# Moving the first stages of an attention and FFN kernel: products of zeros first, Q by head pairs, sums ahead of V, and loads issued later

## The chip, the cores and the metric

The kernel runs on one core of a Trainium2 chip. The metric is the device time of one execution in microseconds (us). The span of an execution (first to last instruction of the program) is 1.7 to 2.2 us shorter than its time.

## The reference, cut to what matters

```python
# q, k, v: (batch 8, heads 8, sequence 1024, head_dim 64); E, F: (64, 1024)
k_proj = np.einsum('ks,bhsd->bhkd', E, k)
v_proj = np.einsum('ks,bhsd->bhkd', F, v)
scores = scale * np.matmul(q, k_proj.transpose(0, 1, 3, 2))
attn = softmax(scores)                       # over the 64 projected positions
x = np.matmul(attn, v_proj)                  # reshaped to (8192 tokens, 512)
h = np.maximum(x @ w_in, 0.0)                # w_in: (512, 2048)
return h * h @ w_out                         # w_out: (2048, 512)
```

The attention is cheap and the FFN is large. The change touches only how batch 0 gets from the first load to the first FFN matmul.

## The kernel before: the parts that the change and the argument touch

All loads of K, Q, V, `w_in` and `w_out` are issued by GpSimd on one queue. The issue order is K, Q, V in three pieces, and then the weights. The first block of `w_in` comes in two pieces, `n = 0` and `n = 1`.

```python
for s in (slice(0, 4), slice(4, 8)):
    load_heads(K_first, k, s)
load_q_half(0, slice(0, H))
for s in (slice(0, 4), slice(4, 6), slice(6, 8)):
    load_heads(V_first, v, s)
# ... (cut)
for j in (0, 2, 1, 3):
    # ... (cut)
    for g in range(2):
        for n in range(2) if (j, g) == (0, 0) else (slice(None),):
            # ... (cut)
            nc.gpsimd.dma_start(
                w_in_sb[j][:, g, :, s], w_in_view[:, g, :, j * fw:(j + 1) * fw][:, :, s])
```

The first stages of batch 0 run in program order on each engine. The `filler` products are thrown away; they keep TensorE busy.

```python
def first_stages(self):
    def filler(n):                       # needs ET, so runs only once E is transposed
        ps = ffn_psum("ps_fill")
        for _ in range(n):
            nc.tensor.matmul(ps[:], lhsT=ET[:, 0:2, :], rhs=ET[:], start=True, stop=True)
    filler(2); self.project_k(0); filler(1); self.transpose_k(0)      # (lines joined here)
    self.project_k(1); filler(2); self.transpose_k(1); filler(1)
    for g in range(2):
        self.half_transpose_q(0, g, ffn_psum)
    for g in range(2):
        self.half_scores(0, g)
        self.half_exponentials(g)
    heads = [slice(0, 4), slice(4, 6), slice(6, 8)]
    self.project_v(heads[0]); self.copy_v(heads[0])
    self.half_sums(0, apart=True); self.half_sums(1)
    self.half_reciprocals(0); self.half_reciprocals(1)
    self.half_values(0)
    for s in heads[1:]:
        self.project_v(s); self.copy_v(s)
    self.half_values(1)
    # ... four normalizes, then the FFN
```

The FFN opens with four steps of four matmuls. Step `cb` needs the piece of x that one normalize writes. Steps 0 and 1 need the first block of `w_in`.

```python
if b == 0 and ch == 0:
    steps[0:4] = [
        lambda cb=cb: opening(range(4), (cb,), cb == NCB - 1) for cb in range(NCB)]
```

The softmax here doesn't subtract the row's maximum and nothing guards it: scores larger than these inputs give would overflow.

## Time and profile before

| before | value | read from |
|---|---|---|
| time | 483.68 us (483.64 to 484.29) | 3 runs |
| span of the profiled run | 482.4 us | the page |
| TensorE busy | 97% of the span | the page |
| first FFN matmul | 21.05 us | the timeline |
| FFN matmul 17 (the first 16 are done) | 24.70 us | the chain in order of time |
| first matmuls of batch 1's K and V | 53.03 and 53.32 us | the timeline |

Read it from the bottom. TensorE is nearly full from 21 us on. The two places where the first stages meet a deadline are the first FFN matmul and the projection of batch 1's K and V.

### The profile page before, as it was taken

To read this page: it belongs to the slowest core of one execution; us is meant where nothing else is said; L and a number is where in the kernel's file an instruction comes from. 1 tells how busy PE (TensorE), PEld (TensorE's weight loads), DVE (VectorE), ACT (ScalarE), POOL (GpSimd) and SP (SyncE) were. 2 spreads that over 40 slices of the span, in tenths; PEclk is the share of its full clock that TensorE was granted. 3 is DMA by queue.
4 is the path that set the end of the run, shared out by engine and by line. 5 is a ranking of instruction groups with operands and counts; after the bars stand their busy time and mean duration, and the time that the engine had idled before them with its cause. 6 is when DMAs were issued, how large, how long until landed. Compare 5 with 4: busy or idle time off the path is not lost.

```text
span 482.4 us, 8423 instructions
## 1 busy us (share of the span) xinstructions
PE 470.3 (97%) x3630; PEld 292.6 (61%) x3630; DVE 314.1 (65%) x382; ACT 261.5 (54%) x413; POOL 34.7 (7%) x48
## 2 busy tenths in 40 slices
PE   4899999999999999999999999999999999999997
PEld 2544676475574746657475665747557474666656
DVE  1478955554958559493776848667494855948383
ACT  2387544758427564466635667176662756545351
POOL 6540020020020001000010000100000000000000
PEclk9999999999999999999999999999999999999999
DMA  9999989579989086941859147690702102020202
GB/s 155 203 204 207 168 181 200 137 120 229 180 128 229 12 175 88 180 94 50 153 86 227 22 115 131 91 200 1 165 11 75 25 1 88 1 88 0 88 1 87
DMA packets 72789, 55.46 MB, mean 115 GB/s; under 512 B 33968, under 2 KB 64944, under 8 KB 72752
## 3 DMA queue, kind: packets, MB, share of 16 engines
q0 software_dynamic: 30624, 29.36, 39.4%
q1 hardware_dynamic: 42128, 25.56, 21.1%
q8 instruction: 28, 0.46, 0.4%
q14 instruction: 9, 0.07, 0.0%
HBM read 59.24 MB, written 16.78 MB: 158 GB/s over the span
## 4 chain that ended last, share of the span: by engine, by line
PE 92%; DVE 3%; DMA 3%; ACT 1%; POOL 1%; issue 0%; POOLq 0%
PE ps_h L459 44%; PE ps_y L479 23%; PE ps_z L479 11%; PE ps_x L479 6%; DMA V_sb<-in_v_dram 3%; PE ps_kv L180 2%; PE ps_att L221 2%; PE ps_att L206 2%; DVE hsq L521 1%; DVE s L473 1%; PE ps_v L284 0%; DVE xT L246 0%; DVE xT L351 0%; PE ps_kv L181 0%; ACT h_relu L513 0%; POOL K_sb L93 0%
## 5 line engine op out<-in xcount | busy, mean ns | idle before, releaser
L459 PE MATMUL ps_h<-xT,w_in 128*128 128x512 bf16 x1024 | 224.8, 379 | 0.2 <-DVE xT L351 0.2
L521 DVE TENSOR_TENSOR hsq<-h_relu 128x1024 bf16<-128x1024 f32 x123 | 149.9, 1222 | 75.0 <-ACT h_relu L513 74.2
L513 ACT ACTIVATE h_relu<-ps_h 128x512 f32<-128x512 f32 x255 | 149.4, 597 | 63.4 <-PE ps_h L459 63.0
L459 PEld LDWEIGHTS <-w_in 128*128 128x128 bf16 x1024 | 99.7, 98 | 117.7 <-issue 1.9
L479 PEld LDWEIGHTS <-s 128*128 128x128 bf16 x1024 | 98.5, 98 | 19.8 <-issue 8.7
L479 PEld LDWEIGHTS <-hsq 128*128 128x128 bf16 x768 | 73.8, 98 | 17.3 <-issue 3.8
L479 PE MATMUL ps_y<-T,s 128*128 128x256 bf16 x512 | 62.4, 273 | 0.0
L246 DVE TENSOR_TENSOR xT<-ps_att,rs 128x1024 bf16<-128x1024 f32 x28 | 33.4, 1215 | 17.6 <-ACT rs L236 17.0
L473 DVE TENSOR_TENSOR s<-hsq 128x1024 bf16<-128x1024 bf16 x64 | 43.5, 683 | 0.0
L591 ACT COPY o_sb<-ps_y 128x512 f32<-128x512 f32 x15 | 8.8, 586 | 53.8 <-PE ps_y L479 53.7
L213 ACT ACTIVATE expT<-ps_att 128x1024 bf16<-128x1024 f32 x28 | 27.2, 1025 | 14.0 <-PE ps_att L206 14.0
L479 PE MATMUL ps_x<-w_out,hsq 128*128 128x256 bf16 x256 | 33.2, 273 | 0.0
L479 PE MATMUL ps_y<-w_out,hsq 128*128 128x256 bf16 x256 | 33.2, 273 | 0.0
L595 DVE TENSOR_TENSOR o_sb<-ps_z,p_b 128x512 f32<-128x512 f32 x16 | 11.0, 688 | 33.8 <-issue 19.9
L479 PE MATMUL ps_y<-T,hsq 128*128 128x256 bf16 x256 | 30.9, 272 | 0.0
L479 PE MATMUL ps_z<-T,s 128*128 128x256 bf16 x256 | 30.6, 273 | 0.0
L479 PE MATMUL ps_z<-w_out,s 128*128 128x256 bf16 x256 | 30.6, 273 | 0.0
L591 ACT COPY p_b<-ps_y 128x512 f32<-128x512 f32 (+1 forms) x17 | 9.4, 556 | 25.9 <-PE ps_y L479 25.8
L81 POOL DMA_DIRECT2D Q_sb<-in_q_dram x7 | 6.1, 876 | 227.7 <-DMA qT<-Q_sb 227.2
L473 DVE TENSOR_TENSOR s<-s,hsq 128x1024 bf16<-128x1024 bf16 x32 | 21.8, 684 | 0.3
L473 DVE TENSOR_TENSOR s<-hsq,s 128x1024 bf16<-128x1024 bf16 x32 | 21.7, 682 | 0.0
L591 ACT COPY p_a<-ps_y 128x512 f32<-128x512 f32 (+1 forms) x17 | 9.4, 561 | 21.8 <-PE ps_y L479 21.6
(75 smaller groups left out, 233.0 us busy)
## 6 DMA issues: line engine op xcount, KB each, us to landing
out_dram<-o_sb SPq DMA_DIRECT2D x30, 512.0 KB, 3.8
K_sb<-in_k_dram POOLq DMA_DIRECT2D x7, 1024.0 KB, 15.3
V_sb<-in_v_dram POOLq DMA_DIRECT2D x7, 1024.0 KB, 22.4
Q_sb<-in_q_dram POOLq DMA_DIRECT2D x7, 1024.0 KB, 9.4
w_out<-in_moe_w_out_dram POOLq DMA_DIRECT2D x4, 512.0 KB, 13.2
w_in<-in_moe_w_in_dram POOLq DMA_DIRECT2D x7, 256.0 KB, 10.0
K_sb<-in_k_dram POOLq DMA_DIRECT2D x2, 512.0 KB, 8.5
out_dram<-o_sb SPq DMA_DIRECT2D x3, 256.0 KB, 2.1
```

What stands on the lines that cost most here:

```text
L180: nc.tensor.matmul(ps[0:KP, :], lhsT=ET[:, i, :], rhs=kv[:, :, i, :], start=f, stop=l)
L206: nc.tensor.matmul(ps[o, bank, :], lhsT=self.kT[r, 2 * pr + j, :], start=True, stop=True, rhs=self.qT[r, NT * (2 * pr + j):NT * (2 * pr + ...
L213: nc.scalar.activation(e[:], self.ps["s", pr][:], AF.Exp, scale=SCALE)
L221: nc.tensor.matmul(ps[32 * j:32 * j + 32, a, :], lhsT=weights(o, 4 * g + j), rhs=self.exp[2 * g + j // 2][o, bank, :], start=True, stop=Tr ...
L246: nc.vector.tensor_tensor(out=self.xT[:, 2 * g + e].rearrange("p a n t -> p a (n t)"), in0=self.ps["v", g, e][:], in1=self.rs[g][:], op=AL ...
L459: nc.tensor.matmul(ps[:], lhsT=w_in_blk(cb, fb), rhs=xT[:, cb, :, 2 * ch:2 * ch + 2], start=(cb == 0), stop=(cb == NCB - 1),)
L473: nc.vector.tensor_tensor(out=s[o][:, js], in0=x, in1=y, op=op)
L479: nc.tensor.matmul(ps[tb] if len(ps) == 2 else ps[0][:, tb], lhsT=lhs[:, j, tb * P:(tb + 1) * P], rhs=rhs[:, j], start=first and n == 0 an ...
L513: nc.scalar.activation(r[:, n], ps[:], AF.Relu)
L521: multiply = lambda: nc.vector.tensor_tensor(out=o, in0=r[:], in1=r[:], op=ALU.mult)
L591: nc.scalar.copy(to[:, t], ps)
L595: nc.vector.tensor_tensor(out=to[:, t], in0=ps, in1=more[:, t], op=ALU.add)
```

## The change

The intent is to have TensorE at full clock before K lands, to keep GpSimd's issues out of the way of VectorE, and to start the FFN before the last values are through. The diff, cut to its core:

```diff
     load_q_half(0, slice(0, H))
-    for s in (slice(0, 4), slice(4, 6), slice(6, 8)):
-        load_heads(V_first, v, s)
+    zeros = const_pool.tile([P, 512], BF16, name="zeros")
+    nc.vector.memset(zeros[:], 0.0)
@@ loads
+    def loads_of_v():
+        nc.gpsimd.tensor_copy(landed[:, 0:1], ET[:, 0, 0:1])     # waits for E's transposes
+        for s in (slice(0, 4), slice(4, 6), slice(6, 8)):
+            load_heads(V_first, v, s)
+    def loads_of_weights(kT):
+        nc.gpsimd.tensor_copy(landed[:, 1:2], kT[:, 0, 0:1])     # waits for kT's first half
+        ... (the loads of w_in and w_out, as before)
+    def filler(n):
+            nc.tensor.matmul(ps[:], lhsT=zeros[:, 0:P], rhs=zeros[:], start=True, stop=True)
@@ first_stages
-            filler(2)
+            filler(3)
             self.project_k(0)
-            filler(1)
+            filler(3)
             self.transpose_k(0)
+            loads_of_weights(self.kT)
             self.project_k(1)
-            filler(2)
+            filler(3)
             self.transpose_k(1)
-            filler(1)
-            for g in range(2):
-                self.half_transpose_q(0, g, ffn_psum)
+            for n in range(4):
+                self.half_transpose_q(
+                    0, range(2 * n, 2 * n + 2), ffn_psum, nc.scalar.copy if n == 1 else nc.vector.tensor_copy)
...
+            self.half_sums(0, apart=True)
             self.project_v(heads[0])
             self.copy_v(heads[0])
-            self.half_sums(0, apart=True)
...
             self.half_values(0)
+            self.half_normalize(0, 0, 0)
             for s in heads[1:]:
...
+        def last_of_first(self):                  # now called after the first FFN step
             self.half_values(1)
@@ main
+        filler(10)
         E_and_F()
+        loads_of_v()
```

## The prediction

> **What bounds the kernel now.** I read the page first, then the chain of waits in order of time, then the timeline of the two places where a load could hold TensorE, and the rates by stretch. Over the whole span the page's chain is TensorE with few breaks:
>
> ```profile
> PE 92%; DVE 3%; DMA 3%; ACT 1%; POOL 1%; issue 0%; POOLq 0%
> ```
>
> Columns of the next view, the chain in order of time: start, duration, work.
>
> ```profile
> 4.21 12.57 DMA V_sb<-in_v_dram
> 16.78 0.04 issue
> 16.82 1.06 PE ps_v L284 x16
> ...
> 19.43 0.66 PE ps_v L284 x16
> 20.09 0.02 issue
> 20.11 0.29 DVE vp L288
> 20.40 0.61 DVE xT L351
> 21.01 0.04 issue
> 21.05 3.61 PE ps_h L459 x16
> 24.67 0.04 issue
> ```
>
> The first 16.8 us are a load: V's first four heads, issued at 4.21, land 12.57 us later. From 19.43 to 21.05 a short serial tail follows (project the last two heads of V, copy, normalize), then the FFN starts. So the diff works on at most the first 21 us; from there TensorE is nearly full.
>
> Is the load late because it is issued late, or because it queues? The stretches (columns: window, length, busy time of PE, PEld, DVE, ACT, POOL, clock, DMA share, GB/s) say the latter:
>
> ```profile
> 4.00:9.00 5.00, 2.21 (x18) 1.29 (x18) 1.11 (x2) 1.63 (x2) 4.02 (x6) 1.00 1.10 163
> 9.00:20.00 11.00, 9.74 (x141) 6.16 (x141) 3.86 (x10) 3.72 (x7) 3.90 (x6) 1.00 1.32 202
> 20.00:50.00 30.00, 29.52 (x219) 13.33 (x216) 24.55 (x31) 21.67 (x37) 8.12 (x11) 1.00 1.26 205
> ```
>
> From 9 to 50 us the loads run at a flat 202 to 205 GB/s, whatever the engines do. By issue plus landing time the order is strictly K, Q, V, w_in: K's halves at 8.7 and 11.6, Q at 14.2, V at 16.8, 18.2, 19.4, w_in from 20.0, each 256 KB taking about 1.27 us. One queue is full all the way.
>
> The decisive lines come much later, where batch 1's K and V are first used:
>
> ```profile
> 30.31 0.88 POOL L81 DMA_DIRECT2D V_sb<-in_v_dram  x1 [0.40 <-PE ps_att L307]
> ...
> 53.03 0.40 PE L180 MATMUL ps_kv<-K_sb,ET 128*64 128x512 bf16 x1
> 53.03 0.11 PEld L181 LDWEIGHTS <-FT 128*64 128x64 bf16 x1
> ...
> 53.32 0.38 PE L181 MATMUL ps_kv<-V_sb,FT 128*64 128x512 bf16 x1
> ```
>
> The tile view gives 23.0 us from issue to landing for that V: 30.31 + 23.0 = 53.3. The weights of V's projection are in the array at 53.03, with K's first matmul, but V's first matmul starts at 53.32. One batch later, where the loads are long done, both start together:
>
> ```profile
> 92.79 0.40 PE L180 MATMUL ps_kv<-K_sb,ET 128*64 128x512 bf16 x1
> 92.79 0.11 PEld L181 LDWEIGHTS <-FT 128*64 128x64 bf16 x1
> 92.79 0.40 PE L181 MATMUL ps_kv<-V_sb,FT 128*64 128x512 bf16 x1
> ```
>
> So at 53.3 us TensorE has just caught up with the load queue and already waits about 0.29 us. Whatever it gains before is waited away here, unless the queue itself gets ahead. That is the step on which I stake the prediction.
>
> **What the Trainium skill says.** (1) "DMA: Bandwidth & Descriptors", section Queues, rings and completion order: on each DMA engine descriptors are consumed in ring order. The trace agrees: loads land in the order of issue. Holding back a later issue then does nothing for an earlier load, as long as the ring does not run dry. (2) "TensorE: Matmul & The Clock Gate", Part 1, the clock gate: TensorE runs at half clock until busy for about 3.4 us. The trace shows the effect: the eight matmuls of K's first half took 1.92 us from 9.11, those of the second half 1.06 us from 12.00. (The granted clock shows as 1.00 throughout, so the durations decide.) (3) "SBUF — State Buffer", section Who interferes with whom: VectorE's two-port copies and GpSimd's descriptor writing share a port, and the later one waits. Compatible: of V's three issues two took about 0.71 us and one 1.02, with VectorE's cast of E from 4.24 to 4.93 beside it.
>
> **The change part by part.**
>
> *Zeros and filler.* Ten 128x512 products before E: cold ones run at roughly 0.43 us (twice the warm 13.81 / 64 = 0.216), so about 4.3 us from near 1.4, after a memset that I estimate at 0.5 us (ones: 0.09 for 32 columns). They end near 5.7, so E's transposes move from 4.98 to about 5.7 and ET from 6.14 to 6.9. K lands only at 8.7: no loss. TensorE is warm for K's first half: 1.92 becomes 1.06, and kT's first half is ready near 11.3 instead of 12.4. But K's second half lands at 11.6 and Q at 14.2, so Q's transposes still start at 14.2 to 14.3. Worth 0.
>
> *V's loads after E, w_in's after kT.* V is issued at about 7 instead of 4.2. The ring holds K and Q until 14.2, so it does not run dry: V lands at 16.8 as before. Seven w_in issues of 0.70 us from about 11.5 are in the ring by about 16.5, before V's last load at 19.4: w_in lands as before. Worth 0. Two one-column GpSimd copies (an estimate, 0.2 us each) are off the path.
>
> *Q by head pairs.* Before, two copies of 128x1024 of 0.69 us, and the first scores at 15.69. After, four of 128x512: 0.42 on VectorE (as ET's copy), 0.59 on ScalarE (as FT's copy). From 14.27: pair 0 done at 15.1, pair 1 (ScalarE) 15.5, pairs 2 and 3 15.6 and 16.0. Scores start at 15.6 and 16.05 instead of 15.69 and 16.29; the exponentials end at 18.0 instead of 18.1. Worth 0.1.
>
> *Sums ahead of V.* V's projection now waits for the first exponentials (17.05) and the sums: 17.2 to 18.3, where it had 16.82 to 17.88. The values come near 18.8 instead of 18.4, still before the reciprocals (near 19.3). Not on the path.
>
> *First FFN step before the last values.* The first normalize (0.62 us) is done near 20.0, so the first four FFN matmuls (0.9 us) start when V's last projection ends, near 20.1, instead of at 21.05, and cover the copy. Then values (0.45), and the 12 other matmuls. The first 16 end at 20.1 + 3.6 + 0.45 + 0.05 = 24.2, against 24.66. The loads allow it, just: w_in's third block lands at 22.1, and its fifth at 24.6 is wanted at 24.65.
>
> Sum on TensorE before 53 us: about 0.45 us earlier. On the span: TensorE reaches batch 1's projection at about 52.6, V lands at 53.3 all the same, the wait grows from 0.29 to about 0.7, and the end moves by 0 to 0.1 us.
>
> **Rivals.** *A, the queue gets faster.* Between 4 and 9 us it moved 163 GB/s, not 203: 5 x 40 KB = 200 KB, 1.0 us. GpSimd issues without a break until 8.0 in that stretch. If that writing slows the transfers, and the later issue cures it, the landing at 53.3 comes forward by up to 1 us and the gain on TensorE counts as well: 482.7 to 483.2. Against: GpSimd is idle from 8 to 9 and the rate is still low, and from 20 to 21.8 it issues without a break at 210 GB/s. *B, TensorE bound after all,* with the reading at 53.3 wrong: 483.68 - 0.45 = 483.2. *C, a new wait.* w_in's issues, back to back, meet VectorE's two-port kp copy at 13.5 and hold it up to 0.7 us, and with it, in order, Q's transposes. Up to +0.5 on the first stages, for which the wait at 53.3 has some 0.7 of room: 483.7. *D, the ring runs dry,* if GpSimd's first copy is very slow (over 5 us before V's issue) or waits for a late ET: +1 to +3. Nothing in the profile speaks for it.
>
> **Range and chances.** Main line 483.6; A and B together have perhaps a third and pull down by 0.5, D is rare. I say 483.5, with 482.9 to 484.2 for eight times in ten; the runs before alone spread from 483.64 to 484.29. Two per cent would be 9.7 us; the touched stretch has 21 us, of which 16.8 are a full queue. Same 0.985, faster 0.008, slower 0.007.
>
> **What would show it.** Right: batch 1's V still lands at about 53.3; its first matmul starts there, with K's first well before it (0.6 us or more); first FFN matmul near 20.1, the first 16 done near 24.2; Q's transposes at 14.3; K's first projection about 1.1 us long. Wrong: V's landing earlier than 53.0 (A), no wait on it at all (B), Q's transposes later than 14.6 (C), a hole in the load rate between 12 and 20 us (D).

## More of the kernel before

All runs told of here count as fast-state runs.

The columns are packets, MB, and share of 16 engines' span.

```profile
q8 instruction: 28, 0.46, 0.4%
```

These are 28 packets of 16 KB that carry instructions. They move 0.46 MB beside 55 MB of data, so they look like nothing.

Executions of one kernel on this core scatter by about 2 us: 43 runs of the kernel before, on several chips, lie between 483.30 and 485.74.

## The result, and the profile after

The changed kernel took 484.81 us (median; 484.31 to 485.01, 6 runs), and the kernel before took 483.81 us (483.52 to 484.58, 6 runs) in the same rounds. The ratio is 1.0016, with a 95% interval of 1.0003 to 1.0029. Ratios here are the mean time of one kernel's fast runs over that of the other's of the same rounds, so not quite the ratio of the medians quoted. A later set of five runs of the unchanged diff gave 484.36 and 1.0005. Taken together, 11 runs after average 484.60 and 43 runs before average 484.10. The change therefore costs about half a microsecond, 0.1%. The time was above the predicted range, and nothing was gained.

Most of that half microsecond lies outside the span, so the profiles here do not show it. Time minus span is 1.71 to 1.81 us in all 37 runs of the kernel before for which it is listed, and 2.09 to 2.16 us in the 11 runs after: 0.36 us more on average, and the two groups do not overlap. The mean spans are 482.35 before and 482.47 after; the 0.12 between them is lost in the scatter. Where the 0.36 us come from was not tested. defer_only (1.78 on average) has none of it, fillers_only and ten_zeros (2.0) have part of it, and every kernel with the new order (2.08 to 2.22 in 50 runs, those of no_filler among them) has it all. What follows explains the two profiled executions, whose spans happen to be 0.45 us apart.

The page's chain is still TensorE, 92% of the span as before. The stretches (columns as in the prediction: window, length, busy time of PE, PEld, DVE, ACT, POOL, clock, DMA share, GB/s) show the same load rate from 9 us on (202 GB/s, and 205 from 20 to 50 us, as before). The view now shows a granted clock below 1:

```profile
4.00:9.00 5.00, 3.67 (x23) 1.66 (x21) 1.11 (x2) 1.63 (x2) 2.60 (x5) 0.86 1.10 160
9.00:20.00 11.00, 9.54 (x133) 6.02 (x134) 4.11 (x11) 4.39 (x8) 5.15 (x9) 0.91 1.31 202
```

This does not mean that the kernel before had the better clock here. The view shows 1.00 until the first change of clock that the trace holds, and in the kernel before that is the rise at 11.2 us; K's first half took 1.92 us there, as at half clock. For the same reason the mean granted clock of a run counts only what is lost after the first rise: no_filler's profiled run has 1.000, although it is at half clock to 23.26 us.

The chain in order of time (start, duration, work) no longer runs through V. It runs through K, kT, the issue of `w_in`, and a piece of `w_in`:

```profile
9.25 1.89 PE ps_k L278 x8
...
12.58 0.18 POOL landed L127
12.77 0.63 POOL w_in L134
13.39 8.20 DMA w_in<-in_moe_w_in_dram
21.59 0.05 issue
21.63 0.60 PE ps_h L476 x2
```

The timeline of TensorE shows what that piece does. The bracket gives the idle time before a line and what ended it.

```profile
20.39 0.61 PE L476 MATMUL ps_h<-xT,w_in 128*128 128x512 bf16 x2
21.63 0.60 PE L476 MATMUL ps_h<-xT,w_in 128*128 128x512 bf16 x2 [0.64 <-DMA w_in<-in_moe_w_in_dram]
22.17 0.41 PE L336 MATMUL ps_att<-expT,vp 64*32 64x256 bf16 x16
22.51 3.69 PE L476 MATMUL ps_h<-xT,w_in 128*128 128x512 bf16 x15
```

The FFN does start earlier, at 20.39 instead of 21.05. Two matmuls later it stands for 0.64 us until the second piece of `w_in`'s first block lands at 21.59. Matmul 17 starts at 25.39 instead of 24.70. At batch 1 the situation is then reversed:

```profile
53.71 0.40 PE L196 MATMUL ps_kv<-K_sb,ET 128*64 128x512 bf16 x1
53.72 0.40 PE L197 MATMUL ps_kv<-V_sb,FT 128*64 128x512 bf16 x1
```

K and V start together. By the landing records V landed at 53.19, so TensorE was late for it and waited for nothing. From there on the two kernels are alike: the last V matmul of that projection starts at 54.82 before and 55.25 after, and the span ends 427.6 us later in both. All of the 0.45 us between the two spans (482.38 and 482.83) is made before 54 us.

**Why was the piece late?** The landing records give, for each load, when its last engine was done. Before, the block's first piece landed at 20.02 and its second at 20.70, 0.68 us apart. After, they landed at 20.24 and 21.59, 1.35 apart. The DMA view of the microsecond before shows one packet that is not data. These are the lines for the kernel before, window 20 to 21 us, with columns packets, MB, share of 16 engines:

```profile
q0 software_dynamic: 209, 0.19, 118.6%
q8 instruction: 1, 0.02, 5.6%
```

And for the changed kernel, window 19 to 20 us:

```profile
q0 software_dynamic: 337, 0.19, 134.0%
q8 instruction: 1, 0.02, 5.6%
```

A share of 5.6% of 16 engines for 1 us is 0.9 us of one engine, while most of the data packets in these two windows hold 512 bytes or 1 KB. The packet starts at 20.55 before and at 19.34 after. It carries the next 16 KB of instructions. The Trainium skill, "Runtime: NRT & Kernel Launch", section Instruction fetch mechanics, says that each engine's instruction store is refilled in 16 KiB blocks of 256 instructions over a DMA queue of its own, and calls the cost "mostly hidden". The trace agrees on the mechanism: later in a trace these packets come roughly every 130 recorded matmuls, each with its weight load, and 28 of them account for 7168 of TensorE's 7260 counted instructions. In the changed kernel this packet falls ahead of the second piece. If it goes to an engine that still owes its part of that piece, the piece is late by about what the packet took. This was the theory after the result. The rivals were that `w_in` is late because it is *issued* late, as the chain above suggests, that the half clock costs the time, and that the deferral itself does.

### The profile page after: what moved, and what is told of

Same layout as the page of the kernel before. It is cut to its first block, busy times and chain, and to the rows that moved or that the text cites. A ratio compares the mean times of both kernels' runs of the same rounds, so it can differ in the third digit from the quotient of the medians.

```text
span 482.8 us, 8456 instructions
## 1 busy us (share of the span) xinstructions
PE 474.5 (98%) x3643; PEld 293.4 (61%) x3643; DVE 314.7 (65%) x384; ACT 262.0 (54%) x414; POOL 34.8 (7%) x50
## 4 chain that ended last, share of the span: by engine, by line
PE 92%; DMA 3%; DVE 3%; ACT 1%; issue 0%; POOL 0%; POOLq 0%
PE ps_h L476 44%; PE ps_y L496 23%; PE ps_z L496 11%; PE ps_x L496 6%; PE ps_kv L196 3%; PE ps_att L237 2%; DMA w_in<-in_moe_w_in_dram 2%; DMA K_sb<-in_k_dram 2%; PE ps_att L222 2%; DVE hsq L538 1%; DVE s L490 1%; DVE xT L262 0%; PE ps_k L278 0%; ACT h_relu L530 0%; DVE xT L367 0%
## 5 line engine op out<-in xcount | busy, mean ns | idle before, releaser
L490 DVE TENSOR_TENSOR s<-hsq,s 128x1024 bf16<-128x1024 bf16 x32 | 21.8, 684 | 0.0
L608 ACT COPY p_a<-ps_y 128x512 f32<-128x512 f32 (+1 forms) x17 | 9.4, 561 | 21.8 <-PE ps_y L496 21.6
```

The lines of the kernel that those rows point to most:

```text
L490: nc.vector.tensor_tensor(out=s[o][:, js], in0=x, in1=y, op=op)
L608: nc.scalar.copy(to[:, t], ps)
```

## The experiments

Twelve runs were made, two of them of the unchanged kernels; all were correct. Each call has its own runs of the kernel before. "Gap" below is the time from the landing of `w_in`'s first piece to that of its second. "Late" is what a piece took beyond the usual distance (0.66 us from first to second piece, 1.27 from second to third).

### First call: each part alone

**loads_early**: the changed kernel with all loads issued as before.

```diff
+    for s in (slice(0, 4), slice(4, 6), slice(6, 8)):
+        load_heads(V_first, v, s)
-            loads_of_weights(self.kT)        # the loads stand where they stood before
-        loads_of_v()
```

> The changed kernel with V's and w_in's loads issued at the start, as in the kernel before. My theory is that the queue of loads is full either way, so the place of issue is worth nothing, and the loss comes from the rest: TensorE's instruction stream is longer by the fillers, its first fetch of the next 16 KB of instructions moves from 20.55 to 19.34 us, lands on a DMA engine in front of the second piece of w_in's first block (landing 21.59 instead of 20.70), and the new order makes the very first FFN step wait for that piece. Theory: still slow, 484.4 to 485.0, w_in's second piece landing later than 21.3. Rival (the deferral makes the loads late): back to 483.7 or below.

Measured: 484.13 us (483.98 to 484.36, 5 runs), ratio 0.9997 (0.9981 to 1.0012). The chain of waits:

```profile
6.42 0.65 POOL w_in L132
7.06 13.69 DMA w_in<-in_moe_w_in_dram
20.75 0.05 issue
20.80 0.60 PE ps_h L475 x2
```

Both figures of the expectation were missed: the time is below 484.4, and the piece landed at 20.75, not after 21.3, since all loads ran earlier here. It is the gap that speaks. The load is issued 6.3 us earlier than in the changed kernel, and the gap is even longer, 2.03 us (fetch at 18.72). So the late issue, which the chain of the changed kernel puts on the path, is not the cause. A chain names the issue that *preceded* a load, not what the load waited for in the queue.

**defer_only**: the kernel before plus the two late issues, `loads_of_v()` and `loads_of_weights(self.kT)`.

```diff
         E_and_F()
+        loads_of_v()
...
             self.transpose_k(0)
+            loads_of_weights(self.kT)
```

> The kernel before with only the loads of V and w_in held back, nothing else. Theory (fetch and new order): within 0.2 us of the kernel before, first fetch still near 20.5. Rival (deferral costs): 0.5 to 1 us slower, V or w_in landing later by as much.

Measured: 484.33 us (483.55 to 485.61), ratio 1.0001 (0.9983 to 1.0018). The gap is 0.69 with the fetch at 21.17, after both pieces, and FFN matmul 3 does not wait. The tile view of `kp` shows the mechanism of rival C (durations are min/median/max in ns):

```profile
L273 DVE COPY kp<-kp x2: 219/337/455, 12.2 to 14.3; 64x256 bf16<-64x256 bf16 x2
```

The second copy takes 0.46 us beside GpSimd's issues instead of the 0.22 of the kernel before; in the changed kernel it is 0.46 too. Q's transposes start 0.78 us after Q landed, partly because of this and partly because K was late in this run. The timed runs cannot tell the deferral's cost from zero.

**no_filler**: the changed kernel without any products of zeros.

```diff
-            filler(3)      # all three, and filler(10) ahead of E
```

> The changed kernel with no products of zeros at all: 19 products, 38 TensorE instructions fewer. Theory: the first instruction fetch comes later (near 20 us or after), beyond w_in's second piece or at least later in it; w_in's second piece lands before 21.1 and the time comes down to 483.6 to 484.2. If the fetch still falls before the piece, the loss stays and the fetch theory is not refuted but not shown. Rival (the new order of the stages or the deferral costs, whatever the fillers): stays at 484.8. Third reading (fillers needed for the clock): slower still.

Measured: 486.60 us (484.53 to 487.87), ratio 1.0044 (1.0023 to 1.0065). TensorE stays at half clock until 23.26 us:

```profile
19.95 1.92 PE L300 MATMUL ps_v<-V_sb,FT 128*64 128x256 bf16 x16
```

V's projection takes 1.92 us instead of 1.06, and FFN matmul 1 starts at 24.09. The profiled run is the slowest of the six (487.87; the fastest took 484.53), so this is the worst case. Some filler is needed, and the kernel before had enough. The fetch comes at 23.35 here, behind the pieces; the gap is 0.66 and nothing waits. From FFN matmul 1 to matmul 17 this kernel takes 4.19 us: that is what the new order needs when no load is late.

**fillers_only**: the kernel before with its products replaced by those of zeros, ten of them ahead of E.

```diff
-            filler(2)  # ET   ->  +            filler(3)  # zeros, and so on as in the change
+        filler(10)
         E_and_F()
```

> The kernel before with only its fillers changed to the 19 products of zeros: 26 TensorE instructions more. Theory: first fetch near 19.4 and w_in's second piece or the block after it lands some 0.6 us later, but the old order wants that piece only about 21.5, so the loss is 0 to 0.5 us: 483.7 to 484.2. Rival (fillers alone cost the whole): 484.6 to 485.

Measured: 484.21 us (483.17 to 485.69), ratio 1.0004 (0.9986 to 1.0022). The fetch comes at 18.34, the gap is 1.88, and the kernel before's own order now waits as well:

```profile
20.50 0.82 PE L461 MATMUL ps_h<-xT,w_in 128*128 128x512 bf16 x3 [0.32 <-DMA w_in<-in_moe_w_in_dram]
```

Thirteen more products, each with its weight load (26 instructions), are enough to move the packet ahead of the piece. The profiled run (span 481.15) was otherwise the fastest of all, because its loads started early.

### Second call: other orders

**after_again** is the changed kernel unchanged, for a second profile.

> The changed kernel unchanged, a second sample of its profile and of its times. The first one showed two things mixed: how soon K's first half lands (9.11 us here, 7.65 to 9.95 over six profiles) and the wait of the first FFN step for the second piece of w_in's first block. Fetch theory: the first fetch again near 19 us, before that piece; the piece lands 1.0 to 2.0 us after the first piece (0.66 to 0.69 where the fetch comes later), and FFN matmul 3 starts right at its landing. Rival (the piece was late by chance): 0.7 us between the pieces and no wait. Queue theory (holding the loads back delays K itself): K's first half again later than 8.5; chance theory: anywhere between 7.6 and 10.

Measured: 484.36 us (484.33 to 484.61, 5 runs), ratio 1.0005 (0.9992 to 1.0017). The fetch is at 18.93, the gap 1.88, FFN matmul 3 waits 0.59 us, and matmul 17 starts 4.96 us after matmul 1 (5.00 in the first profile). The picture repeats. K's first half landed at 8.06, before 8.5, which speaks against the queue theory of the expectation.

**after_reorder**: the last values come between matmul 2 and matmul 3 of the FFN, so that the second piece is wanted later.

```diff
                 steps[0:4] = [
-                    lambda cb=cb: opening(range(4), (cb,), cb == NCB - 1) for cb in range(NCB)]
+                    lambda: opening((0, 1), (0,)), rest,      # rest: the other matmuls of steps 0 and 1
+                    lambda: opening(range(4), (2,)), lambda: opening(range(4), (3,), True)]
```

> The changed kernel, with only the order of the first 16 FFN matmuls altered: matmuls 1 and 2 (which need the first piece) first, then the last values, then 3 and 4 with later ones. Same number of TensorE instructions, same fetch, same loads. Fetch-and-wait theory: matmul 17 comes 0.7 to 0.8 us earlier against V's last landing (4.9 to 5.0 us after it, where it was 5.75), and the time falls by about 0.7 us to 484.0, or less where batch 1's V, some 33.5 us after V's last landing, takes over as the limit. Rival (loss from the deferral or the sums ahead of V): unchanged within 0.2.

Measured: 484.25 us (483.81 to 485.81), ratio 1.0007 (0.9991 to 1.0024). The fetch is at 19.04 and the gap 1.93, as in the changed kernel, but matmul 17 comes 4.27 us after matmul 1 instead of 4.96 to 5.00. Work put into the wait takes it away on TensorE. But the measure set beforehand failed: matmul 17 comes 5.74 us after V's last landing, not 4.9 to 5.0, and 5.74 is the "unchanged" of the rival (5.75 in the first profile). In this profile TensorE was at half clock from 8.00 to 11.41 us, Q's transposes started 0.76 us after Q had landed, and matmul 1 came 1.47 us after V's last piece instead of 0.75. In early_reorder and steady_best, which have this order of matmuls and no such late start, it is 5.15. The span (481.92) profits less: V's first matmul now waits 0.2 us for its landing.

**early_reorder** is after_reorder with the loads issued as before.

```diff
-            loads_of_weights(self.kT)        # on after_reorder: loads as in loads_early
-        loads_of_v()
```

> The same reorder with the loads issued at the start as in the kernel before. Queue theory: K's first half lands near 7.7 (before 8.5), and the time is 1 us below the changed kernel's. Chance theory: K's landing scatters as in the deferred ones, the time is that of the reorder alone. In both VectorE's second copy of kp takes 0.22, not 0.46 us.

Measured: 484.12 us (483.64 to 485.94), ratio 1.0008 (0.999 to 1.0026). In the profiled run TensorE is ahead of everything, and this happens:

```profile
52.42 0.40 PE L196 MATMUL ps_kv<-K_sb,ET 128*64 128x512 bf16 x1
52.97 0.38 PE L197 MATMUL ps_kv<-V_sb,FT 128*64 128x512 bf16 x1
```

FFN matmul 17 is at 23.89, 0.8 earlier than before, but V lands at 52.93, so TensorE waits 0.55 us at V. The span is 482.03 against 482.38. K's first half landed at 8.44, where the queue theory had 7.7, and the time did not fall by 1 us; the second copy of `kp` took 0.22 us, as expected.

**early_reorder_later**: in addition the projection of batch 1 comes two FFN groups later, so that V has landed.

```diff
-        33: "project", 34: "copy_kp, transpose_q, copy_vp", 37: "copy_v_down",
+        35: "project", 36: "copy_kp, transpose_q, copy_vp", 37: "copy_v_down",
```

> As the one before, and batch 1's projection two FFN steps later (about 1.8 us), so that TensorE does not meet batch 1's V while it lands. If that landing is the limit once the first stages are quick, this gains 0.2 to 0.7 us over the one before, the end then follows matmul 17 alone (matmul 17 plus 457.4 us), and it is below both kernels, 482.8 to 483.5. If it is not the limit: no difference.

Measured: 484.40 us (483.70 to 485.92), ratio 1.0012 (0.9996 to 1.0028). V is not waited for (projection at 53.98, V landed at 52.50). The fetch came so early, at 17.86, that it hit the *first* piece: that piece landed 1.75 us after V's last one instead of about 0.65, and FFN matmul 1 waited 0.99 us for it. The profiled span is 481.56; the six runs average 484.61, no better than the kernel before, and the expected 482.8 to 483.5 did not come.

### Third call: chance, fewer instructions, and a steadier clock

**before_again** is the kernel before, unchanged.

> The kernel before, unchanged, for a second profile. Fetch theory (TensorE's next 16 KB of instructions ride on one of the engines that carry the loads): the fetch falls after 20.3 us again, the two pieces of w_in's first block land 0.66 to 0.7 us apart, third FFN matmul not held. Whether early work on TensorE brings the loads of E and F sooner (5.61 to 5.90 us in seven profiles with products of zeros ahead of E, 6.37, 7.10 and 7.77 in three without): if that is cause, F's last piece lands after 6.2 us here and K's first after 8.5; if chance, anywhere from 5.6. The phase of the clock's windows: TensorE warm from somewhere between 10.5 and 12.7 us. Time 483.3 to 485.0, ratio 1.

Measured: 483.78 us (483.58 to 484.68, 4 runs), ratio 1.0002. F's last piece landed at 5.70 us and K's first at 8.18. So F can land early without early work on TensorE. That it is chance alone is not shown: over all 14 profiles F's last piece landed at 5.61 to 5.90 in nine with zeros ahead of E and at 6.56 in the tenth, and at 5.70, 6.37, 7.09 and 7.77 in the four without. The fetch is at 19.85, not after 20.3 as I wrote: the loads, and TensorE with them, ran about 0.8 us earlier here. It missed the second piece (gap 0.63, due just then) and hit the third, which came 2.37 us after the second. The kernel before can pay for the fetch too: matmul 17 starts 3.97 us after matmul 1 instead of 3.65.

**ten_zeros**: the kernel before plus only the ten products ahead of E.

```diff
+        ps = ffn_psum("ps_fill")
+        for _ in range(10):
+            nc.tensor.matmul(ps[:], lhsT=zeros[:, 0:P], rhs=zeros[:], start=True, stop=True)
         E_and_F()
```

> The kernel before with ten products of zeros ahead of E and F and nothing else. If early TensorE work brings E's and F's loads sooner: F's last piece below 6.0 us and K's first heads below 8.5; if chance, F anywhere between 5.6 and 7.8. Fetch theory: about 20 more instructions ahead of w_in's first block, so the fetch comes near 19.5 us instead of 20.55, ahead of the second piece, which then lands 1.3 to 2 us after the first instead of 0.66 to 0.7, and the third FFN matmul waits for it (0.3 to 0.9 us). If instead the fetch has nothing to do with the landing, the pieces land 0.7 us apart wherever the fetch falls. Clock: warm from about 5 to 8 us, then back at half clock for one window because TensorE has less to do than in the kernel with all the products. Time within 0.2% of before under all theories, 483.3 to 484.7.

Measured: 485.23 us (484.79 to 485.39, 4 runs), ratio 1.0027 (1.0014 to 1.004). My figure for the fetch (19.5) was wrong, it was 20.88: K's first heads landed at 9.39 and everything came later. Thus it was no test of an earlier fetch. What it did show fits: the second piece was due with the fetch and was on time (gap 0.60), and the third was 0.63 late. It is the slower of the two kernels with the old order and zeros. In the profile TensorE is at half clock until 13.44 us, and Q's transposes start 0.54 us after Q landed. Whether that is the whole of the 0.27% I did not separate.

**v_in_two**: the changed kernel with V's last four heads as one slice instead of two, which saves 32 TensorE instructions.

```diff
-            heads = [slice(0, 4), slice(4, 6), slice(6, 8)]
+            heads = [slice(0, 4), slice(4, 8)]          # and the loads likewise
```

> The changed kernel with V's last four heads loaded and projected as one slice instead of two: 32 fewer TensorE instructions ahead of the FFN. Fetch theory: the fetch moves behind about 20.3 us, the second piece of w_in's first block lands 0.66 to 0.7 us after the first, the third FFN matmul does not wait, and the time from the start of the last V projection matmul to FFN matmul 17 is 4.3 to 4.5 us instead of 5.1 (no fetch inside the loads) although V's projection itself ends up to 0.5 us later. If the fetch is not what delays the piece, that gap stays 1.3 to 2 us and FFN matmul 3 waits 0.4 to 0.9 us. Time: FFN matmul 17 near 24.6 to 25.2, so span 482.0 to 482.6 and 483.9 to 484.6 us: 0 to 0.5 below the changed kernel.

Measured: 484.67 us (483.70 to 484.88, 4 runs), ratio 1.0018 (1.0004 to 1.0033). In absolute time the fetch came at 19.16, since all loads ran earlier in this profile, so that part of the expectation failed. Relative to the last V projection matmul it moved from 0.73 to 0.89 us ahead (the two profiles of the changed kernel) to 0.59 ahead. The gap fell to 0.66, and the third piece took the delay (1.84 us after the second instead of 1.27). Nothing waits for a load now:

```profile
19.95 1.04 PE L476 MATMUL ps_h<-xT,w_in 128*128 128x512 bf16 x4
20.92 0.41 PE L336 MATMUL ps_att<-expT,vp 64*32 64x256 bf16 x16
21.27 3.90 PE L476 MATMUL ps_h<-xT,w_in 128*128 128x512 bf16 x16
```

From matmul 1 to matmul 17 it takes 4.19 us, exactly as without filler, and 0.8 less than the changed kernel. From the last V projection matmul to matmul 17 it is 4.39, inside the expected 4.3 to 4.5, but in part by luck: the expectation wanted the fetch behind the pieces, and here it started 0.72 us before the second one landed and did not delay it. The time does not show the gain. The profiled run is the fastest of the four, and the other three are as slow as the changed kernel.

**steady_best** is early_reorder_later with four products of zeros between E and F, to keep the granted clock up, and two instead of three ahead of K.

```diff
             copy(t[:], ps[:])
+            if t is ET:
+                filler(4)
...
-            filler(3)
+            filler(2)
             self.project_k(0)
```

> The best of the reordered kernels (loads issued early, zeros, the step of sums moved back, w_in's pieces one place later) with four of the zero products between E and F, and two instead of three ahead of K. If the clock's fall-back in the slow tail (granted 0.992, spans near 483.7) comes from a gap on TensorE between E and K, the tail goes: every run between 482.7 and 484.2, span 480.6 to 481.8, ratio 0.997 to 0.999. If the tail is the chip's own scatter of start-up and of the clock's windows, runs spread over 483.5 to 486 as with the others and the ratio is 1.000 to 1.001: no order of the first 25 us beats the kernel before by over 0.3%.

Measured: 484.20 us (483.66 to 485.74, 6 runs), ratio 1.0012 (1.0000 to 1.0024). The clock part worked: no run has a mean granted clock below 0.999. In the nine other sets with zeros ahead of E (the first six runs of the changed kernel among them), 28 of 48 runs are at 0.996 or below. The time part did not: one run still took 485.74 at a full clock. So the tail of slow runs is not only the clock's. Part of it goes with the clock: of those 48 runs, the 20 above 0.996 average 484.27 us, the 22 at 0.996 484.49, and the five at 0.992 took 485.69 to 485.94. No version tried beats the kernel before.

### The fetch and the late piece, in all profiles

All times are in us. The fetch time is the start of the first instruction packet. "Due" for a late piece is the landing before it plus 0.66 (second piece), 1.27 (third) or 0.65 (first, after V's last).

| profile | fetch | first piece | second | third | late piece, by |
|---|---|---|---|---|---|
| before | 20.55 | 20.02 | 20.70 | 22.05 | none (third: 0.08) |
| defer_only | 21.17 | 20.29 | 20.98 | 22.26 | none |
| no_filler | 23.35 | 20.97 | 21.63 | 22.89 | none |
| before_again | 19.85 | 19.29 | 19.92 | 22.29 | third, 1.10 |
| ten_zeros | 20.88 | 20.45 | 21.05 | 22.95 | third, 0.63 |
| v_in_two | 19.16 | 19.22 | 19.88 | 21.72 | third, 0.57 |
| after | 19.34 | 20.24 | 21.59 | 22.50 | second, 0.69 |
| after_again | 18.93 | 19.09 | 20.97 | 21.91 | second, 1.22 |
| after_reorder | 19.04 | 19.18 | 21.11 | 22.01 | second, 1.27 |
| loads_early | 18.72 | 18.72 | 20.75 | 21.74 | second, 1.37 |
| fillers_only | 18.34 | 18.57 | 20.45 | 21.28 | second, 1.22 |
| early_reorder | 18.59 | 19.45 | 20.83 | 21.91 | second, 0.72 |
| steady_best | 19.07 | 19.90 | 21.26 | 22.37 | second, 0.70 |
| early_reorder_later | 17.86 | 19.97 | 20.34 | 21.47 | first, 1.10 |

No piece is late without a fetch ahead of it. A fetch is followed by a late piece in 11 of the 13 profiles where it falls before the third piece has landed. It was harmless in two, before and defer_only. I take it that there the packet fell on an engine that was ahead of the others. The trace as I could read it does not name the engine of a packet, so that this is the mechanism remains argued; shown is only that the late piece comes after the fetch. Six of the 11 pieces are late by more than the packet itself took (0.89 to 0.98 us), so its own time is not the whole of the delay.

## Why the prediction was wrong, point by point

**The load queue is first in, first out, and late issues are worth nothing: right in substance.** The rate from 9 us on is 202 to 205 GB/s in both kernels, and V's last piece lands 10.5 to 10.7 us after K's first in the two first profiles. Rivals A and D are out.

**Zeros and filler, "Worth 0": right that they gain nothing, wrong in the reason.** The step "TensorE is warm for K's first half: 1.92 becomes 1.06" failed. K's first half took 1.89 us at 9.25. These stretches of the changed kernel (columns as above; the clock is the third number from the end) show why:

```profile
4.30:7.60 3.30, 1.97 (x20) 1.24 (x17) 1.11 (x2) 1.04 (x1) 1.20 (x4) 1.00 1.07 162
7.60:11.10 3.50, 3.34 (x14) 1.56 (x13) 0.00 (x0) 0.59 (x1) 1.10 (x2) 0.51 1.20 182
```

The clock came up at 4.2 us and fell back for 3.4 us, although TensorE had been busy for 1.97 of the 3.30 us before (1.26 of them with transposes of E and F). Where Q landed late this cost nothing (Q's transposes start 0.04 us after its landing, in the first profile). Where Q landed early, it held Q's transposes back by 0.62 us (after_again). It does not always happen: of the ten profiles with zeros ahead of E, five show this fall-back, and in four of these Q's transposes start 0.62 to 0.90 us after Q's landing. In four (fillers_only, early_reorder, early_reorder_later and steady_best) the clock first came up at 5.08 to 5.70 us instead of 4.07 to 4.85 and stayed up; there K's first half took about 1.05 us, as predicted, and the transposes start within 0.05 us. ten_zeros, without the later products, came up at 13.44 only.

**Sums ahead of V, "Not on the path": wrong when the loads are early.** In six profiles with the new order and zeros (all but early_reorder_later, where the fetch hit the first piece, and v_in_two, which has a shorter V), the first FFN matmul comes 5.89 or 5.90 us after Q's transposes begin, whenever V lands. The chain includes 0.72 us in which TensorE waits for the first exponentials. In the old order the same matmul comes 1.66 or 1.67 us after V's last piece (before, before_again, fillers_only; 1.71 and 2.02 in ten_zeros and defer_only, where Q's transposes started late). So the new order is bound by Q where the old one was bound by V. Since V's last piece lands about 5.15 us after Q (14.24 to 19.39 before), the new order can be at most 5.15 + 1.66 - 5.90 = 0.9 us earlier at the first matmul. From matmul 1 to 17 it needs 4.19 instead of 3.65, because the values now lie in between. The gain on TensorE was at most 0.9 - 0.54, roughly 0.4 us, near the predicted 0.45.

**First FFN step before the last values: this is the step that failed.** "The loads allow it, just" was worked out for the third and fifth piece. The second was not looked at, and by the prediction's own numbers it did not fit: matmul 3 would come at 20.1 + 2 x 0.216 = 20.53, and the piece landed at 20.70 before. In its place the runs show a second piece that lands late behind a fetch of 16 KB (1.35 and 1.88 us after the first piece, instead of 0.68): the mis-sized term is matmul 1 to matmul 17, predicted as 20.1 to 24.2 (4.1), measured as 5.00 and 4.96. Without the hit it is 4.19 (v_in_two, no_filler). In the first profile part of the wait was there anyway: without the fetch the piece was due at 20.24 + 0.66 = 20.90, and matmul 3 would have come at about 20.82, two products of 0.216 after 20.39. So about 0.1 us of the 0.8 belongs to a tight load and 0.7 to the fetch.

**The staked step, "batch 1's V lands at 53.3 whatever", with the gain waited away: right as a ceiling, but not what bound.** V landed at 53.19. TensorE came at 53.71, after it, not before it. That a gain would have been waited away is shown by early_reorder, which stood 0.55 us at V. The prediction was thus asymmetric without saying so: it reckoned what a gain is worth there (0 to 0.1), and never asked what a *loss* is worth. A loss counts in full once it exceeds the 0.29 us that TensorE waited. From the landing of V's last piece to matmul 17 it was 5.31 us before and 5.75 after, a loss of 0.44. The landings differ by 0.25 for reasons of start-up. Of the sum of 0.69, the old wait with its restart absorbs 0.24: the span grew by 0.45.

**The step from span to time, which the prediction took as fixed.** "The end moves by 0 to 0.1 us" is a statement on the span, and it was carried over to the time. The runs show time minus span 0.36 us longer after the change. In the averages this is most of the loss, and its cause stays open.

**Rival C** was right in mechanism and smaller than said: the `kp` copy took 0.24 us longer, not up to 0.7, and in the first profile Q's landing hid it. **Rival B** (TensorE bound after all) came true with the opposite sign. Among the arguments against rival A, "at 210 GB/s" is a misreading: the view for 20 to 21.8 us has 205, which changes nothing.

**The range** was 482.9 to 484.2, while the runs of the kernel before turned out to spread from 483.30 to 485.74. Three runs within 0.65 us had made the scatter look smaller than it is.

What stays open: what the 0.36 us outside the span are; whether the late issue of the loads costs anything in time (the intervals of loads_early and defer_only leave room for 0.19% either way). What starts the loads up to 2 us earlier or later in one execution than in another is also open. So is why the fetch comes after some 130 to 143 recorded matmuls in the new order and after 168 to 174 in the old; these counts include the products, so the added products do not explain it.

## What to carry to other kernels

Where a matmul follows a load with a few tenths of a microsecond to spare, look in the DMA view for instruction packets nearby: here the late pieces came behind one, and added products moved it. Put work that needs no load between two such matmuls, as after_reorder does, rather than trust the landing to the tenth. When one wait caps what a change can gain, work out what the change costs if it turns out slower, because a loss is not capped. And compare time minus span between two kernels before explaining a difference in time from their profiles.

## What the Trainium skill lacked or had wrong

- "Runtime: NRT & Kernel Launch", section Instruction fetch mechanics: crossing a 16 KiB block is called mostly hidden. TensorE itself was not seen to starve, but a load of data landed 0.57 to 1.37 us late behind the fetch in 11 profiles, which held the FFN by up to 0.64 us in the changed kernel and 0.99 in early_reorder_later. That loads can land late behind a fetch (a packet of about 0.9 us) should stand there; by what mechanism is not shown here.
- "TensorE: Matmul & The Clock Gate", Part 1: the clock is said to drop after an idle window of about 3.4 us. Here it dropped after a window in which TensorE was busy for 1.97 of 3.30 us. But 1.26 of these were transposes, which Part 4 of the same page does not count as busy in the same way, so the page is not shown to be wrong. What it lacks is how much work short of a full window keeps the clock up: in steady_best, with four more products of 512 columns in that stretch, it did not drop in any of six runs. The length of the slow stretch, 7.64 to 11.06 us, agrees with the page.
- No page that I read has the start-up of the first loads: K's first heads landed between 7.65 and 9.95 us over the 14 profiles, which is more than the change was meant to win.
